# Clustered attention with a Mish FFN: clusters assigned for four heads at once, with block transposes on VectorE and one constant product, and all bulk loads on one queue

## The chip, the cores and the metric

The kernel runs on one core of one Trainium2 chip. The metric is the device time of one execution in microseconds; lower is better. Five engines work beside each other, each through its own list of instructions in order: PE (TensorE, with PEld its weight loads), DVE (VectorE), ACT (ScalarE), POOL (GpSimd) and SP (SyncE, which here only issues DMA transfers). ACT issues DMA transfers too.

## What is computed

Four batches of eight heads, 768 positions, head dimension 64. Each query and key is assigned to one of 16 clusters of its head (largest cosine with a centroid, the first one on a tie); a query attends only to keys of its own cluster. The heads' outputs are joined and go through a two-layer FFN with Mish.

```python
B, H, S, D = q.shape                      # 4, 8, 768, 64
q_assign = np.argmax(np.einsum('bhsd,hcd->bhsc', q_n, c_n), axis=-1)   # 16 clusters
k_assign = np.argmax(np.einsum('bhsd,hcd->bhsc', k_n, c_n), axis=-1)
mask = q_assign[:, :, :, None] == k_assign[:, :, None, :]
scores = np.where(mask, scale * np.matmul(q, k.transpose(0, 1, 3, 2)), -1e9)
attn = softmax(scores)                    # float32 throughout
x = np.matmul(attn, v)                    # -> (3072, 512)
h = x @ w_in                              # 512 -> 2048
g = h * np.tanh(softplus(h))
out = g @ w_out                           # 2048 -> 512
```

`q_n`, `k_n` and `c_n` are the rows divided by their norms.

## The kernel before, in words

**Units.** A head of a batch is numbered n = 0 to 31. Its 768 queries are done in three units of 256, so there are 96 units; unit i has two halves a = 0, 1 of 128 queries. For one half, `scores` makes a 128x768 tile `s` in PSUM (two banks, two buffers with the tag "S"), `rowmax` reduces it on DVE, `expo` takes the exponential on ACT with its sum `l`, `recip` inverts the sum. For the first 24 units (batch 0) `p_lo` transposes P in fp32 on TensorE (tiles `q`, copied to `pt`) and `pv` multiplies with V in fp32 (L588 into 64-column strips of `o`, and L600, which spreads the sums). Later units split P in two fp16 parts (`hl`: POOL L539, DVE L556), transpose them with DMA transposes on SP (`pt`<-`hl`), and L588 is fp16. `pv` does two units at once, each in one half of the array's columns. `pv_out` writes the result to tiles `x`, two fp16 parts.

**FFN.** A step j (of 96) of `m1` makes `h` = w_in-part x `x` (L649 to L651, 24 products of 256 columns), `e_mish`, `e_gh`, `e_gl` make `g`, and `m2` accumulates `O` (L687 to L689, 512 columns). FFN step j stands about 25 units behind attention unit j.

**Weights.** 32 loads (`w_load`, tiles `stage`) bring 64-bit values; ACT (L239) and DVE (L248, L249) turn them into fp32 (`w_abs`, `w_f32`), TensorE sums squares (`w_sq`, tile `gram`), and ACT, POOL and DVE split them in fp16 parts. All this is done during the first 24 units.

**Operands of a head.** `qk_load` brings the raw tile `qk` (128x768: 64 rows of q and 64 of k, 384 KB); `prep_hi` and `prep_lo` scale it (POOL L373, in place) and split it in `A` and `B`; `copy_t`, `copy_z`, `copy_b`, `copy_a` move halves of these into place, by ACT, DVE or DMA. The operands `Z` and `T` have 80 rows: 64 of values and 16 of one-hot clusters, so that the product L493 adds a huge negative number where the clusters differ. These 16 rows are what the change is about.

**The assignment before**, once per head. `assign_mm` (L426): six fp32 products per head, each with a 128x128 piece of the raw tile as the stationary operand and 32 columns of the centroid matrix `C` as the moving one; `C` has for each head 16 columns that see k and 16 that see q. `assign_hot`: DVE takes the maximum of each 16 (L446), compares (L447), a product with `desc` (16 down to 1, POOL or DVE, L453) and a second maximum and compare (L454, L456) leave the first of equal ones. `assign_put`: six bf16 transposes on TensorE (L462), then one ACT instruction (L470) writes the staging tile `stg`, from which `hot_copy` takes the 16 rows to `Z` and to `T` by DMA. For heads 0 and 1 the rows are written directly (L466, L467). The tile "oh" of the transposes is a PSUM buffer that it shares with `o`.

**What sets the order.** A planner (`Plan`) sorts all steps by a time from a table `T` (in units); `pl.after` draws a step's predecessors ahead. Afterwards a scheduler with an estimated timeline sets each engine's list, so that the diff alone doesn't show the order. Bulk loads go to SP or ACT by a fraction in the table (`queue`): all `qk` loads, the w_out stages and half of the w_in stages are issued by ACT.

Of the kernel before, what the change touches and what calls it, by code (L numbers as in the profile page):

```python
# [15 lines left out]
ALU = mybir.AluOpType  # L16
# [39 lines left out]
def tile_clustered_attention_mish_ffn(  # L56
# [13 lines left out]
    raw = pool("raw", 2)  # L70
# [7 lines left out]
    xp = pool("x", 21)  # L78
    mp = pool("moe", 2)
    gp = pool("g", 1)  # L80
    sm = pool("small", 4)
# [11 lines left out]
    def queue(n, kind):  # L93

        f = T["dq", kind]
        if kind == "stage" and n < 8:
            return nc.sync
        return nc.scalar if int((n + 1) * f) != int(n * f) else nc.sync

    last = []  # L100
# [14 lines left out]
    NG, NU, NJ = B * H, B * H * 3, 96  # L115
    units = [(g, qb, g) for g in range(NG) for qb in range(3)]
    uid = {(g, qb): i for i, (g, qb, _) in enumerate(units)}
    first = {}
    for i, (_, _, n) in enumerate(units):
        first.setdefault(n, i)  # L120

# [3 lines left out]
    identb = cp.tile([P, P], BF16, name="identb")  # L125
    nc.vector.tensor_copy(identb, ident)
    ones = cp.tile([P, P], F32, name="ones")
    nc.vector.memset(ones, 1.0)
    desc = cp.tile([P, NCL], F32, name="desc")
    for i in range(NCL):  # L130
        nc.gpsimd.memset(desc[:, i : i + 1], float(NCL - i))
    msc = cp.tile([64, 1], F32, name="msc")
    mbi = cp.tile([64, 1], F32, name="mbi")
    nc.vector.memset(msc[0:32], 1.0)
    nc.vector.memset(msc[32:64], BIG)
    nc.vector.memset(mbi[0:32], 0.0)
    nc.vector.memset(mbi[32:64], -BIG)
# [3 lines left out]
    onehot = [cp.tile([P, 6, 64], BF16, name=f"onehot{i}") for i in range(2)]  # L141
    for o in onehot:
        nc.vector.memset(o, 0.0)


# [34 lines left out]
    def norm_scale(sums, name, pool, tag, largest=False):  # L180
# [5 lines left out]
        if largest:  # L186
# [3 lines left out]
            nc.tensor.matmul(tp[:, :1], ones[:1], m[:1], start=True, stop=True)  # L190
        else:
            nc.tensor.matmul(tp[:, :1], ones, m, start=True, stop=True)
# [20 lines left out]
    def w_load(n):  # L213
# [6 lines left out]
        if i < 8:  # L220
            queue(n, "stage").dma_start(
# [3 lines left out]
        else:  # L225
            r = (n - 16) * P
            queue(n, "stage").dma_start(dst, w_out[r : r + P, :])
# [74 lines left out]
    def v_load(b, hp):  # L302
        t = vp.tile([P, S], F32, tag="v", name=f"vraw{b}_{hp}")
        queue(b * 4 + hp, "v").dma_start(t, vP[b, hp])
        vst[b, hp, "raw"] = t

# [14 lines left out]
    def v_split(b, hp):  # L321
        pl.after(("v_scale", b), ("v_load", b, hp))
        t = vst[b, hp, "raw"]
        if b == 0:
            vst[b, hp] = t.rearrange("p (c h d) -> p c h d", c=6, h=2)
            return
# [37 lines left out]
    def qk_load(n):  # L364
        t = raw.tile([P, S], F32, tag="qk", name=f"qk{n}")
        queue(n, "raw").dma_start(t, qk[n // H, n % H])
        st["qk", n] = t

    def prep_hi(n):
        pl.after(("qk_load", n))  # L370
        r, A = st["qk", n], operand(n, "A")
        if share(n, "f_b", n >= H):
            nc.gpsimd.tensor_scalar(r, r, scq, 1.0, op0=ALU.mult, op1=ALU.mult)  # L373
        sc = 1.0 if share(n, "f_b", n >= H) else scq
        if share(n, "f_a", n >= H):
# [4 lines left out]
    def prep_lo(n):  # L380
        pl.after(("prep_hi", n))
        r, A, Bt = st["qk", n], st["A", n].bitcast(F32), operand(n, "B")
        if share(n, "f_b", n >= H):
# [4 lines left out]
    def copy(n, kind, dst, src):  # L388
# [6 lines left out]
        elif share(n, f"f_{kind}", n >= H):  # L395
# [20 lines left out]
    def assign_mm(n):  # L416
        pl.after(("centroids",), ("qk_load", n))
        h = n % H
        if share(n, "as_o", n >= H):
            o = [ps.tile([P, 512], F32, tag="H", name=f"as{n}_{e}", bufs=2) for e in range(2)]  # L420
        else:
            t = ps2.tile([P, 1024], F32, tag="S", name=f"as{n}")
            o = [t[:, :512], t[:, 512:]]
            st["as", n] = t
        for c in range(6):
            nc.tensor.matmul(  # L426
                o[c // 4][:, c % 4 * P : c % 4 * P + 32], st["qk", n][:, c * P : (c + 1) * P],
                C[:, 32 * h : 32 * h + 32], start=True, stop=True,
            )
        if share(n, "as_o", n >= H):  # L430
            st["as", n] = o

    def assign_hot(n):
        pl.after(("assign_mm", n))
        if n > 1:
# [498 lines left out]
```

## Time and profile before

| what | us |
|---|---|
| median of 3 runs | 992.38 |
| lowest and highest run | 991.54, 995.91 |
| span of the profiled execution | 988.0 |
| the profiled execution's own time | not listed beside its span |
| TensorE busy | 922.7 (93%) |
| VectorE busy | 648.4 (66%) |
| ScalarE busy | 541.3 (55%) |
| GpSimd busy | 430.8 (44%) |

The span is from the first to the last instruction on the core. "Busy" adds up instructions as recorded; those of TensorE are pipelined, so their recorded durations overlap, and what one costs is better read from the distance between two starts. The granted clock is the share of TensorE's full speed that it was given; over the whole span it is 0.976.

### The profile page before, as it was taken

Reading aid. Unit: us, or ns where it says so; the run is one execution under the profiler, and the core shown is the slowest. Engines: PE = TensorE matmul, PEld = TensorE weight load, DVE = VectorE, ACT = ScalarE, POOL = GpSimd, SP = SyncE. Lnnn points to the kernel's source line nnn. Section 1 sums busy time; section 2 is a strip of 40 time slices with the busy share of each in tenths; the row PEclk is TensorE's granted clock in tenths of the full one; section 3 lists DMA queues with packets and bytes.
Section 4 is the critical chain, followed back from the end, with each engine's and each line's share of the span. In section 5 each row is a group of like instructions: output and inputs, shape, how many; then the busy total and the mean of one; then the engine's idle time right before and its main releaser. Section 6 shows DMA issues by size and latency. Waiting matters only on the chain.

```text
span 988.0 us, 17976 instructions
## 1 busy us (share of the span) xinstructions
PE 922.7 (93%) x6913; PEld 665.3 (67%) x6913; DVE 648.4 (66%) x1149; ACT 541.3 (55%) x898; POOL 430.8 (44%) x539
## 2 busy tenths in 40 slices
PE   4998779898999999999999999899999999999997
PEld 3766456676777766767677767667777767676764
DVE  5897976887777767867767777767776776211010
ACT  3676375775666656476756647557566565211111
POOL 3335785426645444654444544644454433111010
PEclk9899788999999999999999999999999999999999
DMA  9735522137796766668577766667657656200000
GB/s 358 227 88 152 175 60 53 39 89 133 134 164 119 157 126 111 130 144 158 116 147 144 149 138 125 125 136 141 134 112 135 118 106 114 43 12 22 12 11 21
DMA packets 250164, 115.49 MB, mean 117 GB/s; under 512 B 229600, under 2 KB 229600, under 8 KB 250080
## 3 DMA queue, kind: packets, MB, share of 16 engines
q1 hardware_dynamic: 238272, 82.50, 43.2%
q10 hardware_dynamic: 11808, 31.86, 11.4%
q8 instruction: 54, 0.88, 0.4%
q14 instruction: 30, 0.25, 0.1%
HBM read 35.68 MB, written 6.29 MB: 42 GB/s over the span
## 4 chain that ended last, share of the span: by engine, by line
PE 22%; ACT 8%; issue 7%; DVE 7%; POOL 5%; DMA 1%; ACTq 0%; POOLq 0%; SPq 0%
PE O L689 3%; PE O L687 3%; PE O L688 3%; PE h L650 3%; PE h L651 3%; PE h L649 3%; POOL hl L539 3%; ACT p L510 2%; DVE m L503 2%; DVE hl L556 2%; ACT u L659 2%; PE o L588 1%; ACT L510 1%; ACT L659 1%; PE s L488 1%
## 5 line engine op out<-in xcount | busy, mean ns | idle before, releaser
L510 ACT ACTIVATE p<-s,m 128x768 f32<-128x768 f32 x192 | 172.7, 900 | 163.7 <-DVE m L503 126.2
L649 PE MATMUL h<-x,w 128*128 128x256 f16 x768 | 212.0, 276 | 2.8 <-ACT x L617 1.5
L650 PE MATMUL h<-x,w 128*128 128x256 f16 x768 | 211.4, 275 | 0.3 <-DVE x L618 0.3
L651 PE MATMUL h<-x,w 128*128 128x256 f16 x768 | 211.5, 275 | 0.0
L556 DVE SCALAR_TENSOR_TENSOR hl<-p,l,hl 128x768 f16<-128x768 f32 x144 | 160.2, 1116 | 61.3 <-POOL hl L539 60.5
L503 DVE TENSOR_REDUCE m<-s 128x1 f32<-128x768 f32 x192 | 181.3, 947 | 18.4 <-PE s L493 16.1
L539 POOL TENSOR_SCALAR hl<-p,l 128x768 f16<-128x768 f32 x144 | 132.4, 921 | 123.9 <-DVE l L521 54.0
L671 DVE SCALAR_TENSOR_TENSOR g<-u,mscg,g 128x512 f16<-128x512 f32 x96 | 78.4, 821 | 132.2 <-POOL g L663 131.3
L663 POOL TENSOR_SCALAR g<-u,mscg 128x512 f16<-128x512 f32 x96 | 79.7, 832 | 177.9 <-ACT u L659 149.1
L687 PE MATMUL O<-w,g 128*128 128x512 f16 x384 | 146.2, 381 | 3.4 <-POOL g L663 2.6
L689 PE MATMUL O<-w,g 128*128 128x512 f16 x384 | 145.8, 380 | 0.9 <-DVE g L671 0.5
L688 PE MATMUL O<-w,g 128*128 128x512 f16 x384 | 145.7, 379 | 0.0
L488 PE MATMUL s<-A,B 128*128 128x384 f32 x384 | 124.6, 406 | 14.9 <-ACT p L510 14.0
L659 ACT ACTIVATE u<-h,msch 128x512 f32<-128x512 f32 x96 | 65.3, 686 | 96.7 <-PE h L651 95.4
L520 POOL TENSOR_SCALAR l<-l 128x1 f32<-128x1 f32 x129 | 43.0, 333 | 170.9 <-ACT p L510 167.5
L493 PE MATMUL s<-Z,T 80*128 80x384 f32 x384 | 103.1, 351 | 3.4 <-ACT T L467 2.5
L649 PEld LDWEIGHTS <-w 128*128 128x128 f16 x768 | 75.9, 99 | 23.8 <-issue 8.4
L488 PEld LDWEIGHTS s<-A,B 128*128 128x128 f32 x384 | 64.4, 195 | 39.1 <-ACT p L510 21.6
L650 PEld LDWEIGHTS <-w 128*128 128x128 f16 x768 | 75.8, 99 | 19.3 <-issue 3.7
L651 PEld LDWEIGHTS <-w 128*128 128x128 f16 x768 | 75.7, 99 | 16.1 <-issue 4.7
L588 PE MATMUL o<-pt,v 128*64 128x256 f16 x1296 | 81.3, 274 | 0.0
L588 PEld LDWEIGHTS <-v 128*64 128x64 f16 x1296 | 68.2, 110 | 14.5 <-issue 12.9
(185 smaller groups left out, 1318.9 us busy)
## 6 DMA issues: line engine op xcount, KB each, us to landing
qk<-in_qk_dram ACTq DMA_DIRECT2D x32, 384.0 KB, 4.2
stage<-in_w_out_dram ACTq DMA_DIRECT2D x16, 512.0 KB, 4.5
vraw<-in_vP_dram SPq DMA_DIRECT2D x16, 384.0 KB, 4.0
out_dram<-osb SPq DMA_DIRECT2D x24, 256.0 KB, 2.3
B<-T ACTq DMA_DIRECT2D x30, 192.0 KB, 4.0
A<-A SPq DMA_DIRECT2D x25, 192.0 KB, 4.6
stage<-in_w_in_dram SPq DMA_DIRECT2D x8, 512.0 KB, 9.4
stage<-in_w_in_dram ACTq DMA_DIRECT2D x8, 512.0 KB, 4.6
```

The lines of the kernel that those rows point to most:

```text
L488: nc.tensor.matmul(s[:, j, :384], st["B", n][:, q0 : q0 + P], st["A", n][:, j * 384 : (j + 1) * 384], start=True, stop=False,)
L503: nc.vector.tensor_reduce(m, st["s", i, a][:, :, :384], axis=AX.XY, op=ALU.max, negate=True)
L510: in_turn(nc.scalar.activation(p.rearrange("p (n x) -> p n x", n=2), st["s", i, a][:, :, :384], AF.Exp, bias=st["m", i, a], scale=1.0, acc ...
L539: nc.gpsimd.tensor_scalar(t[:, 0], p, r, 1.0, op0=ALU.mult, op1=ALU.mult)
L556: nc.vector.scalar_tensor_tensor(t[:, 1], p, r, t[:, 0], op0=ALU.mult, op1=ALU.subtract)
L588: nc.tensor.matmul(o[s * D : s * D + D, :256], v if parts == 1 else v[:, int(part == 1)], st["pt", 2 * m + s][:, :, c + (6 if part == 2 el ...
L649: nc.tensor.matmul(o, wh, xh, start=(c == 0), stop=False)
L650: nc.tensor.matmul(o, wh, xl, start=False, stop=False)
L651: nc.tensor.matmul(o, wl, xh, start=False, stop=(c == 3))
L687: nc.tensor.matmul(o, gh, wh, start=(f == 0 and fi == 0), stop=False)
L688: nc.tensor.matmul(o, gh, wl, start=False, stop=False)
L689: nc.tensor.matmul(o, gl, wh, start=False, stop=(f == 7 and fi == 1))
```

## The change

The assignment is done for a quad of four heads (8 quads instead of 32 heads).

- `assign_mm(q)`: the centroids are now stationary, 32 columns for each of the four heads, in four strips of 32 columns of the array; the raw tiles are the moving operand, 512 and 256 columns. The result has clusters on partitions and positions along the row. So four raw tiles have to be there at once (`raw` has 4 buffers instead of 2), and POOL's scaling in place of these tiles has to wait for the quad's products.
- `assign_hot(q)`: DVE transposes 32x32 blocks, reduces and compares over 48 groups of 16, and transposes the 0/1 result back.
- `assign_put(q)`: one bf16 product with a constant 128x128 matrix `put_w` subtracts the ones of lower index in each group, which leaves the first of equal ones, and scales; DVE takes the maximum with 0 and subtracts `put_b`. `stg` now holds the rows of four heads. `desc`, `onehot`, `msc`, `mbi` and the direct writes for heads 0 and 1 are gone.
- Both PSUM results take a buffer with the tag "S", and the transposed values a buffer of P (`pp`). The staging tile has one buffer, so the last DVE step of a quad waits until the last head of the quad before has been copied.
- `bulk`: all loads of `qk`, `v` and weights are issued by SP, in the order of the plan.
- `pv` waits for V's load instead of its scale in batch 0; the buffers of `x` go from 21 to 18, those of `l` from 12 to 10. The plan's table has new times for the operands' steps. Code for two passes over batch 0 is added and not used (`passes` is 1); with it the unit list, FFN pace and late heads are as before.

```diff
-    raw = pool("raw", 2)
+    raw = pool("raw", T["raw"])
-    xp = pool("x", 21)
+    xp = pool("x", T["xbufs"])
...
+    def bulk(dst, src):
+        made = nc.sync.dma_start(dst, src)
+        if loads:
+            tc.add_manual_dep(made.ins, loads[0], ..., reason="load order")
+        loads[:] = [made.ins.name]
...
+    def put_consts():
+        w = gp.tile([P, P], F32, tag="g", name="put_f")
+        nc.vector.memset(w, -1.0)
...
+        nc.vector.tensor_tensor(w, w, ident, op=ALU.add)
+        nc.vector.tensor_scalar(w4[:, :, 0], w4[:, :, 0], BIG, None, op0=ALU.mult)
+        nc.vector.tensor_copy(put_w, w)
...
-    def assign_mm(n):
-        for c in range(6):
-            nc.tensor.matmul(
-                o[c // 4][:, c % 4 * P : c % 4 * P + 32], st["qk", n][:, c * P : (c + 1) * P],
-                C[:, 32 * h : 32 * h + 32], start=True, stop=True,
+    def assign_mm(q):
+        pl.after(("centroids",), *(("qk_load", n0 + j) for j in range(4)))
+        o = ps2.tile([P, 1024], F32, tag="S", name=f"as{q}")
+        for c0, c1 in ((0, 512), (512, S)):
+            for j in range(4):
+                nc.tensor.matmul(
+                    o[32 * j : 32 * j + 32, c0:c1], C[:, 32 * h : 32 * h + 32], st["qk", n0 + j][:, c0:c1],
+                    start=True, stop=True, skip_group_check=True,
...
+    def assign_hot(q):
+        d = pp.tile([P, S], F32, tag="p", name=f"D{q}")
+        nc.vector.transpose(d, st["as", q][:, :S])
+        nc.vector.tensor_reduce(m, v, axis=AX.X, op=ALU.max)
+        nc.vector.tensor_tensor(hot..., v, m..., op=ALU.is_equal)
+        nc.vector.transpose(t, hot)
+    def assign_put(q):
+        o = ps2.tile([P, 1024], F32, tag="S", name=f"put{q}")
+        for c0, c1 in ((0, 512), (512, S)):
+            nc.tensor.matmul(o[:, c0:c1], put_w, st["hott", q][:, c0:c1], start=True, stop=True)
+        stg = op1.tile([P, S], F32R, tag="stg", name=f"stg{q}")
+        nc.vector.tensor_scalar(stg, o[:, :S], 0.0, put_b, op0=ALU.max, op1=ALU.subtract)
     def qk_load(n):
-        queue(n, "raw").dma_start(t, qk[n // H, n % H])
+        bulk(t, qk[gof[n] // H, gof[n] % H])
...
+    for q, n in owner.items():
+        t = -12 if q == 0 else T["assign1"] if q == 1 and d == 1 else first[n] + T["assign"] * d
```

Where it moves instructions: first TensorE in the stage where attention and FFN run together, at heads 16 and 17 before. `as16` is the assignment product of head 16 (head 16's first piece stands a little earlier), `oh16` its transposes, `s` are scores, `o` is P·V.

```order
L588 MATMUL o20_4379<-pt41_4121,v1_2_2519 64x256
L426 MATMUL as16_4480<-C_142,qk16_4478 128x32 x5
L488 MATMUL s44_1_4487<-A_14_3882,B_14_3897 128x384 x2
L493 MATMUL s44_1_4487<-Z_14_3899,T_14_3885 128x384 x2
...
L426 MATMUL as17_4804<-C_142,qk17_4802 128x32 x3
L462 LDWEIGHTS onehot0_138
L462 MATMUL oh16_4744<-identb_108,onehot0_138 64x128
```

And TensorE at the same heads now: `as4` is the product of the quad of heads 16 to 19, `put4` the constant product, between steps of the FFN (`O`, `h`).

```order
L717 MATMUL O1_1_3797<-w13_1157,g6_3540 128x512
L453 MATMUL as4_4072<-qk16_3984,C_118 32x512
L453 MATMUL as4_4072<-qk17_4066,C_118 32x512
L453 MATMUL as4_4072<-qk18_4068,C_118 32x512
L453 MATMUL as4_4072<-qk19_4070,C_118 32x512
L453 MATMUL as4_4072<-qk16_3984,C_118 32x256
...
L478 MATMUL put4_4212<-hott4_4113,put_w_113 128x512
L478 LDWEIGHTS put_w_113
L478 MATMUL put4_4212<-hott4_4113,put_w_113 128x256
```

One group of eight products and one of two serve four heads, where each head had its own six and six.

Second, ACT while the w_out weights are prepared, before: the `stage` loads stand in its list between the exponentials (`p`), and each waits for its buffer.

```order
L239 ACTIVATE w12_1163<-stage23_1087 128x512
L470 ACTIVATE stg4_1218<-oh4_1211,mbi_130,msc_129 64x768
L227 DMA stage24_1110<-in_w_out_dram 128x512
L227 DMA stage25_1134<-in_w_out_dram 128x512
L227 DMA stage26_1171<-in_w_out_dram 128x512
L239 ACTIVATE w13_1231<-stage24_1110 128x512
L510 ACTIVATE p10_1_1249,l10_1_1250<-s10_1_1242,m10_1_1247 128x768
```

The same loads now, in SP's list, among copies of the heads' operands (`Z`, `T`, `A`).

```order
L108 DMA stage23_1026<-in_w_out_dram 128x512
L108 DMA stage24_1048<-in_w_out_dram 128x512
L108 DMA stage25_1074<-in_w_out_dram 128x512
L108 DMA stage26_1113<-in_w_out_dram 128x512
L108 DMA stage27_1153<-in_w_out_dram 128x512
L493 DMA Z_5_1367<-stg1_939 16x768
L494 DMA T_5_1365<-stg1_939 16x768
```

A load that waits now holds up the copies behind it on SP, no longer ACT's exponentials. Third, SP later, where attention and FFN run together: a raw load stands between the DMA transposes of P.

```order
L587 DMA_TRANSPOSE pt25_2255<-hl25_0_2252 128x12x128
L587 DMA_TRANSPOSE pt25_2255<-hl25_1_2269 128x12x128
L108 DMA qk14_2817<-in_qk_dram 128x768
L587 DMA_TRANSPOSE pt26_2353<-hl26_0_2347 128x12x128
L587 DMA_TRANSPOSE pt26_2353<-hl26_1_2367 128x12x128
```

Before, these raw loads were issued by ACT.

More of the change, by code (lines that the diff above doesn't have):

```diff
@@ L97, in queue @@
             return nc.sync
+        if kind in ("hot", "copy_a", "copy_b") and n < T["act_q"]:
+            return nc.scalar
         return nc.scalar if int((n + 1) * f) != int(n * f) else nc.sync
-    last = []
+    last, loads = [], []
+    def bulk(dst, src):
+        made = nc.sync.dma_start(dst, src)
+        if loads:
+            tc.add_manual_dep(
+                made.ins, loads[0],
+                mybir.DependencyInfo(mybir.DependencyClass.NoSync, mybir.DependencyReason.DATA),
+                reason="load order",
+            )
+        loads[:] = [made.ins.name]
     def in_turn(made):
@@ L117, in tile_clustered_attention_mish_ffn @@
+    gof = {n: g for g, _, n in units}
     uid = {(g, qb): i for i, (g, qb, _) in enumerate(units)}
     first = {}
+    count = {}
     for i, (_, _, n) in enumerate(units):
         first.setdefault(n, i)
+        count[n] = count.get(n, 0) + 1
     ident = cp.tile([P, P], F32, name="ident")
     make_identity(nc, ident)
-    identb = cp.tile([P, P], BF16, name="identb")
-    nc.vector.tensor_copy(identb, ident)
-    ones = cp.tile([P, P], F32, name="ones")
+    ones = cp.tile([P, 1], F32, name="ones")
@@ L128, in tile_clustered_attention_mish_ffn @@
     nc.vector.memset(ones, 1.0)
[L129 to L137, printed above, removed]
+    put_w = cp.tile([P, P], BF16, name="put_w")
+    put_b = cp.tile([P, 1], F32, name="put_b")
@@ L220, in w_load @@
         if i < 8:
-            queue(n, "stage").dma_start(
+            bulk(
                 dst.rearrange("p (c f) -> p c f", c=2),
@@ L226, in w_load @@
             r = (n - 16) * P
-            queue(n, "stage").dma_start(dst, w_out[r : r + P, :])
+            bulk(dst, w_out[r : r + P, :])
     def w_abs(n):
@@ L482, in scores @@
+    def hot_copy(n):
+        q, j = divmod(gof[n], 4)
+        again = T["passes"] == 2 and H <= n < 2 * H
+        pl.after(("assign_put", q), ("copy_t", n), ("copy_z", n))
+        stg, eng = st["kept", q] if again else st["stg", q].bitcast(F32), queue(n, "hot")
+        r = 32 * j
+        eng.dma_start(st["Z", n][D : D + NCL].bitcast(F32), stg[r : r + NCL])
+        eng.dma_start(st["T", n][D : D + NCL].bitcast(F32), stg[r + NCL : r + 2 * NCL])
     def scores(i, a):
@@ L609, in pv_out @@
         b, h = divmod(g, H)
+        if mode(i, 0) == 3:
+            pl.after(("v_scale", b))
         r, r2 = i % 2 * D, h % 2 * D
@@ L806 @@
 T = {
+    'assign1': 2.0,
+    'load1': -2.0,
+    'ffn': [(0, 25.4, 1.0)],
+    'wide': 24,
+    'passes': 1,
+    'v_s0': 30.0,
+    'act_q': 3,
+    'xbufs': 18,
+    'v_sq': 0.5,
+    'assign': -1.4,
+    'lead0': 0.0,
+    'hot_copy': -0.5,
+    'copy_a': -0.57,
+    'copy_b': -0.57,
+    'copy_z': -0.7,
+    'copy_t': -0.73,
+    'prep_lo': -0.8,
+    'prep_hi': -0.87,
+    'load': -1.75,
+    'raw': 4,
     ('f_ws', 0): 0.5,
@@ L846 @@
     ('w_l', 1): 0.7772,
-    'v0': 1.5,
+    'v0': 0.5,
     'v_d': 0.4275,
@@ L867 @@
     'O': 1,
-    'off0': 25.401,
-    'pace': 1.0,
-    ('span', 0): 1.1575,
-    ('span', 1): 1.0762,
-    ('load', 0): -3.8837,
-    ('load', 1): 2.8855,
     ('w0', 0): 0.89,
@@ L883 @@
     ('ws_d', 1): 1.2087,
-    'assign': 0.2164,
-    'hot': 2.2946,
-    'put': 2.3669,
     ('scores', 0): 0.4,
```

217 lines of the change are left out of this document (96 added, 121 removed).

## The prediction

> **What bounds the kernel now.** I read the page's first lines, then cut the span at the first and the last instruction that mix the two halves of the program, then asked in each piece who makes TensorE wait.
>
> ```profile
> span 988.0 us, 17976 instructions
> PE 922.7 (93%) x6913; PEld 665.3 (67%) x6913; DVE 648.4 (66%) x1149; ACT 541.3 (55%) x898; POOL 430.8 (44%) x539
> ```
>
> The cuts are the first FFN product and the last attention product P·V (the first and last starts in these two rows, the second one ending at 853.5):
>
> ```profile
> L649 PE MATMUL h<-x,w x768: 268/273/437, 218.0 to 968.7; 128*128 128x256 f16 x192
> ...
> L588 PE MATMUL o<-pt,v x1296: 272/273/298, 231.3 to 853.2; 128*64 128x256 f16 x186
> ```
>
> ```profile
> 0.00:218.00 218.00, 177.32 (x1167) 132.53 (x1167) 174.99 (x360) 133.17 (x257) 109.49 (x148) 0.91 0.46 140
> 218.00:853.50 635.50, 616.31 (x4883) 448.40 (x4882) 454.44 (x765) 386.78 (x610) 305.44 (x369) 0.99 0.69 131
> 853.50:988.00 134.50, 129.11 (x867) 84.36 (x866) 18.94 (x26) 21.36 (x32) 15.85 (x23) 1.00 0.04 14
> ```
>
> The columns after the length are PE, PEld, DVE, ACT and POOL busy time, then granted clock. Stage A (218 us) is the first 26 units of attention with the preparation of the weights; stage B (635.5) is attention and FFN together; stage C (134.5) is FFN alone. In B TensorE is 97% busy, DVE 72%, ACT 61%, and the longest sum that anything makes TensorE wait there is this:
>
> ```profile
> PE s L488 <- ACT p L510: 11.1, 14, 3.0
> ```
>
> So B is as long as its TensorE work, A is a chain in which DVE is 80% busy and TensorE still idles, and C is untouched by the change.
>
> **TensorE in stage B: the main term.** The old assignment costs what lies between the start of its first product and the start of the next instruction:
>
> ```profile
> 679.60 0.38 PE L689 MATMUL O<-w,g 128*128 128x512 f16 x1
> 679.82 1.42 PE L426 MATMUL as<-C,qk 128*128 128x32 f32 x12
> 681.07 0.59 PE L488 MATMUL s<-A,B 128*128 128x384 f32 x2
> ...
> 515.10 0.52 PE L462 MATMUL oh<-identb,onehot 128*64 128x128 bf16 x6
> 515.55 0.28 PE L650 MATMUL h<-x,w 128*128 128x256 f16 x1
> ```
>
> One head takes 681.07 − 679.82 = 1.25 us for the six fp32 products (two records each) and 515.55 − 515.10 = 0.45 us for the six transposes: 1.70 us. How many heads fall in B:
>
> ```profile
> L426 PE MATMUL as<-C,qk 128*128 128x32 f32 x264 | 32.9, 270 | 0.0
> ```
>
> 264 / 12 = 22 heads, so 22 × 1.70 = 37.4 us leave B.
>
> What comes instead: quads 3 to 7 stand in B by the order of the program, five of eight. Per quad there are eight fp32 products that stream 512 or 256 columns against 32 stationary columns, four strips of the array side by side, and one bf16 product over 768 columns. No row shows four strips. Two strips are shown, by the fp32 P·V of the early units:
>
> ```profile
> 62.05 0.86 PE L588 MATMUL o<-pt,vraw 128*64 128x256 f32 x5
> 62.54 0.38 PE L600 MATMUL o<-ident,l 128*64 128x128 f32 x2
> ...
> 62.76 0.59 PE L600 MATMUL o<-ident,l 128*64 128x128 f32 x4
> ...
> 73.27 1.51 PE L588 MATMUL o<-pt,vraw 128*64 128x256 f32 x12
> 74.72 0.62 PE L488 MATMUL s<-A,B 128*128 128x384 f32 x2
> ```
>
> At 62.5 products of L600 on one strip start while those of L588 run on the other, each strip at its own pace: strips are independent. And 12 records of 256 columns take 74.72 − 73.27 = 1.45 us in two strips, so a record on its strip takes 2 × 1.45 / 12 = 0.24 us for 256 columns. A strip of the new assignment has two records over 768 columns, 2 × 3 × 0.24 = 1.45 us, and if four strips run beside each other that is the quad's time. If only two do, 2.9; if none, 5.8. I take 1.45, because the rows show strips that do not wait for one another, and keep 5.8 as the bad end. The bf16 product costs by L689 above (0.22 us per 512 columns) 0.33. Turning the array from full width to strips and back:
>
> ```profile
> 505.75 0.38 PE L689 MATMUL O<-w,g 128*128 128x512 f16 x1
> 506.06 2.16 PE L588 MATMUL o<-pt,v 128*64 128x256 f16 x36
> 508.15 0.62 PE L488 MATMUL s<-A,B 128*128 128x384 f32 x2
> ```
>
> L588 starts 0.31 us after L689 where 0.22 is its stream, so a turn costs 0.1, two per quad 0.2. Sum per quad 1.45 + 0.33 + 0.2 ≈ 2.0; five quads 10 us. B loses 37.4 − 10 = 27.4 us of TensorE work. TensorE is not quite all of B (97%), and a shorter unit shows a little more of the wait for the exponential; I count nine tenths: −25 us. With two strips at a time it would be 0.9 × (37.4 − 17) = −18, with none −5.
>
> The Trainium skill, "TensorEngine Tiling (Array Packing)", section Key Properties, speaks against the change here: switching the tiling mode drains the array. By the rows above the trace agrees, and the drain is the 0.1 us; the sum would be 1 us better without it. The skill's "TensorE: Matmul & The Clock Gate", section Measured speedup vs the span model, gives 3.07 times for four packed tiles instead of 4; no run here shows it, and by it an estimate of the quad's products is 1.9 us, 2 us more over B.
>
> **The other engines in B.** POOL's product with `desc`, ACT's staging write and DVE's two reduces, compare and one-hot go:
>
> ```profile
> 0.00:218.00 218.00, 19.09 (x40) 0.91 0.46 140
> 218.00:853.50 635.50, 39.88 (x88) 0.99 0.69 131
> ```
>
> This is DVE's time on the tile of maxima (x4 per head): 1.8 us a head in B, 1.9 in A. Per quad DVE now makes two block transposes, a reduce, a compare and the final max-and-subtract, five passes over 128x768. A reduce of that shape is a row; no block transpose is:
>
> ```profile
> L503 DVE TENSOR_REDUCE m<-s 128x1 f32<-128x768 f32 x51 | 48.1, 951 | 15.0 <-PE s L493 13.4 <-ACT rb L627 1.1
> ```
>
> I take 0.95 for all five, 4.75 us a quad (transposes between the same 0.95 and twice it, 6.65 a quad). In B DVE goes from 39.9 to 24 us; it has 28% free there, so nothing is counted. The quad's chain runs about four units ahead of the first scores that need it.
>
> The Trainium skill, "VectorE: DVE Perf Modes", section The three transpose paths, states 311 ns for a 128×128 bf16 transpose on this engine. Six of these are an estimate of 1.9 us per transpose, the upper end above; by it stage A below would be 5 us longer, and the forecast 964 instead of 959.5. No row here shows it.
>
> **Stage A.** Three terms. First the start, which gets longer:
>
> ```profile
> 0.74 0.40 SPq L151 DMA_DIRECT2D csb<-in_cent_dram  x1
> ...
> 3.20 0.22 DVE L154 TENSOR_TENSOR csq<-csb 128x64 f32<-128x64 f32 x1 [0.78 <-DMA csb<-in_cent_dram]
> ...
> 9.47 0.28 DVE L177 COPY C<-ct 64x128 f32<-64x128 f32 x1
> ...
> 21.73 0.96 DVE L503 TENSOR_REDUCE m<-s 128x1 f32<-128x768 f32 x1 [2.89 <-PE s L493]
> ```
>
> ```profile
> GB/s 358 227 88 152 175 60 53 39 89 133 134 164 119 157 126 111 130 144 158 116 147 144 149 138 125 125 136 141 134 112 135 118 106 114 43 12 22 12 11 21
> ```
>
> Now the centroids are the fifth transfer on SP, behind four loads of 384 KB. At 358 GB/s these take 4.4 us, so the centroids land near 6.5 instead of 3.2, and C is ready 6.6 us later (3.20 to 9.75 above), at 13.1. The first products run at half clock (the same twelve records take twice the time of those at 679.82):
>
> ```profile
> 9.90 2.74 PE L426 MATMUL as<-C,qk 128*128 128x32 f32 x12 [0.77 <-DVE C L177]
> ```
>
> So the four strips take 2.9, DVE's four passes 3.9, the product and the last pass 1.6, the copy by DMA about 2.5: 24.0, and two products later the first maximum, near 25.5, against 21.73. POOL comes to the same time: it now scales the raw tiles in place after the assignment has read them, four passes, then A, A and B:
>
> ```profile
> 4.48 0.90 POOL L373 TENSOR_SCALAR qk<-qk,scq 128x768 f32<-128x768 f32 x1 [2.68 <-DMA qk<-in_qk_dram]
> 5.48 0.83 POOL L376 TENSOR_SCALAR A<-qk 128x768 fp32r<-128x768 f32 x1
> 6.39 1.80 POOL L384 TENSOR_TENSOR B<-qk,A 128x768 fp32r<-128x768 f32 x1
> ```
>
> 16 + 3.6 + 1.7 + 1.8 = 23, and the copies after it. So +4.
>
> Second, DVE has three quads to do instead of ten heads: 3 × 4.75 = 14.3 against 19.1 + 1.9 for the two direct copies that also go, −7 on the engine that is 80% busy in A.
>
> Third, the bulk loads leave ACT's queue, where they wait for a staging buffer and hold up what stands behind them:
>
> ```profile
> 100.95 5.88 ACTq L227 DMA_DIRECT2D stage<-in_w_out_dram  x3
> 107.17 0.67 ACT L239 ACTIVATE w<-stage 128x512 f32<-128x512 f32 x1 [5.64 <-DVE w L249]
> ```
>
> Here ACT stands 5.6 us at its own issue while DVE empties the buffer; the exponentials wait behind it. DVE is the slow one at that place, so most of this stays as DVE's time; I count −5. TensorE in A has 10 × 1.7 us less and 3 × 2 more, hidden while DVE leads. A: +4 − 7 − 5 = −8. C: 0.
>
> **Sum.** −25 − 8 = −33 on the profiled execution: 988 − 33 = 955. Its time outside the span isn't listed; the median of the runs, 992.4, lies 4.4 above the span, and I carry that over: 959.5.
>
> **The edits at no cost.** The deeper buffers for raw tiles only let four be held. Eighteen x buffers instead of 21: 12 tiles of a batch live until FFN has read the first third, about 8 units after the batch ends, when the next batch has written six: 18, just enough; without that cover `pv_out` waits one FFN step, 5 us, once a batch. Hot copies for the first three heads go by ACT's queue, which is idle at the start.
>
> **Rivals.** (1) SP's queue makes it slower. The raw loads now stand among the transposes of P:
>
> ```profile
> DMA to landing us min/median/max: 3.6/4.0/7.4
> ...
> L366 ACTq DMA_DIRECT2D qk<-in_qk_dram x20: 329/334/362, 238.4 to 737.8; - x20
> ```
>
> The first row is the landing time of the transposes. 20 loads fall in B; a transpose behind one of them can land one landing later, and what the load waits for holds the queue. It eats the gain when each load holds TensorE for 33 / 20 = 1.65 us; at half a landing, 2 us, plus the waits before it, say 3.5 in all, it is 20 × 3.5 = 70 − 33: about 1030, and just past the point 995 to 1005. For it: the queue is in order. Against it: TensorE waits for no P transpose in the waits of B. (2) The strips don't run beside each other: −5 in B, −8 + 5 in A (two of A's three quads at full clock): 984. Against it: the rows at 62.5. (3) The work leaves but the time doesn't: DVE and the exponential, which make TensorE wait already, take up what it is given, and the start costs what A wins. Then B gives a fifth, −5, A 0: 987 to 992. Against it: 28% of DVE free in B.
>
> **Chances.** My forecast, 948 to 973 (two strips at a time 967; A without its two gains 971; all of B's work, a start no longer than now and twice the gain on ACT's queue, 27 + 17, 948): 0.80. Strips one by one, 984: 0.07. Given back, 987 to 992: 0.06. SP's queue, over 997: 0.07. To hold 8 in 10 the range runs from 946 to 981. Half a per cent, 5 us, is what a measurement of this kernel can tell from none; so faster 0.87 (the first two), same 0.06, slower 0.07.
>
> **What would show it.** Right: the first FFN product near 210; B near 610 with TensorE still 97% busy; eight assignment products of a quad within 1.6 us; C at 134.5; the first maximum near 25. Wrong: products of four strips that start one after another by their full length; TensorE waiting for P's transposes or for Z and T; DVE transposes of several us; ACT or DVE above 90% in B.

## The result and the profile after

The changed kernel takes 983.37 us (median of 4 runs, 982.15 to 984.35), the kernel before 992.99 (4 runs beside it). The ratio is 0.9898 with a 95% interval of 0.9864 to 0.9932: faster by 1.0%, where 3.3% (959.5 us) was forecast. The profiled execution has a span of 981.9 us.

The first lines of its page:

```profile
span 981.9 us, 16957 instructions
PE 890.0 (91%) x6481; PEld 616.4 (63%) x6481; DVE 650.7 (66%) x1052; ACT 515.8 (53%) x866; POOL 423.7 (43%) x498
```

TensorE's busy time is 32.7 us shorter (922.7 before), the span 6.1. The cuts of the stages, from the groups of the first FFN product and of P·V (the last start and its 0.2 us give 847.3):

```profile
L677 PE MATMUL h<-x,w x768: 269/273/421, 221.4 to 962.5; 128*128 128x256 f16 x192
L604 PE MATMUL o<-pt,v x1296: 269/273/423, 234.9 to 847.1; 128*64 128x256 f16 x186
```

The windows of the three stages (PE, PEld, DVE, ACT and POOL busy, then granted clock, DMA share, GB/s):

```profile
0.00:221.40 221.40, 166.43 (x1043) 117.57 (x1044) 171.84 (x330) 125.85 (x245) 106.39 (x128) 0.85 0.45 141
221.40:847.30 625.90, 594.45 (x4574) 414.35 (x4572) 459.87 (x698) 368.59 (x589) 301.42 (x347) 0.98 0.69 132
847.30:981.90 134.60, 129.15 (x867) 84.49 (x866) 19.00 (x26) 21.36 (x32) 15.91 (x23) 1.00 0.04 15
```

| stage | before | forecast | after |
|---|---|---|---|
| A | 218.0 | 210 | 221.4 |
| B | 635.5 | 610 | 625.9 |
| C | 134.5 | 134.5 | 134.6 |

A is 11 us longer than its forecast and 3 longer than before; B is 16 us longer than its forecast and 10 shorter than before. The granted clock in A is 0.91 before and 0.85 now; by x1, x14 and x15 below this is not what A lost. In B TensorE's busy time fell by 21.9 us, but its idle time rose from 635.5 − 616.3 = 19.2 to 625.9 − 594.5 = 31.4. None of the four signs that the prediction names for being wrong appeared: the strips, P's transposes, the DVE transposes and the busy shares of ACT and DVE in B (59% and 73%) are all on the side that it took for right. TensorE's waits in B: the longest is the one of before (11.1 us then), the second has grown (1.3 then), and for P's transposes it waits 0.4 us:

```profile
PE s L503 <- ACT p L525: 16.0, 18, 2.7
PE h L677 <- ACT u L687: 6.8, 9, 1.0
...
PE o L604 <- DMA pt<-hl: 0.4, 1, 0.4
```

The quad itself: the second one, in stage A, at full clock (timeline rows of TensorE and DVE):

```profile
71.92 1.50 PE L453 MATMUL as<-qk,C 128*32 128x512 f32 x16 [0.53 <-ACT p L525]
81.73 0.97 DVE L462 STREAM_TRANSPOSE D<-as 128x768 f32<-128x768 f32 x1
85.56 0.95 DVE L467 TENSOR_TENSOR hot<-D,Dm 128x768 bf16<-128x768 f32 x1
88.57 0.50 PE L478 MATMUL put<-hott,put_w 128*128 128x512 bf16 x2
89.11 1.02 DVE L480 TENSOR_SCALAR stg<-put,put_b 128x768 fp32r<-128x768 f32 x1 [0.34 <-PE put L478]
```

Eight products (16 records) take 1.50 us, so the four strips do run beside each other; the transpose takes 0.97 us. What the forecast has no term for is the 8.3 us between the end of the products (73.42) and the transpose (81.73), and in that time the PSUM buffer of `as` is one that the scores don't have. The third quad, the last in A, has the same gap with 6.3 us; the first, at the start of the kernel, has 0.1. In the five quads of B it is 3.0 to 4.4 us.

```profile
177.37 1.50 PE L453 MATMUL as<-qk,C 128*32 128x512 f32 x16
185.22 0.97 DVE L462 STREAM_TRANSPOSE D<-as 128x768 f32<-128x768 f32 x1
```

### The profile page after: what moved, and what is told of

Its sections match the earlier page's. It is cut to its first block, busy times and chain, and to the rows that moved or that the text cites. A ratio compares the mean times of both kernels' runs of the same rounds, so it can differ in the third digit from the quotient of the medians.

```text
span 981.9 us, 16957 instructions
## 1 busy us (share of the span) xinstructions
PE 890.0 (91%) x6481; PEld 616.4 (63%) x6481; DVE 650.7 (66%) x1052; ACT 515.8 (53%) x866; POOL 423.7 (43%) x498
## 5 line engine op out<-in xcount | busy, mean ns | idle before, releaser
L571 DVE SCALAR_TENSOR_TENSOR hl<-p,l,hl 128x768 f16<-128x768 f32 x144 | 173.2, 1206 | 60.2 <-POOL hl L554 58.7
L554 POOL TENSOR_SCALAR hl<-p,l 128x768 f16<-128x768 f32 x144 | 135.4, 942 | 125.3 <-DVE l L536 41.5
L699 DVE SCALAR_TENSOR_TENSOR g<-u,mscg,g 128x512 f16<-128x512 f32 x96 | 81.8, 856 | 129.4 <-POOL g L691 128.9
L503 PE MATMUL s<-A,B 128*128 128x384 f32 x384 | 128.8, 418 | 25.4 <-ACT p L525 17.5
L535 POOL TENSOR_SCALAR l<-l 128x1 f32<-128x1 f32 x129 | 49.8, 386 | 167.8 <-ACT p L525 162.7
L508 PE MATMUL s<-Z,T 80*128 80x384 f32 x384 | 105.8, 358 | 0.0
L604 PE MATMUL o<-pt,v 128*64 128x256 f16 x1296 | 85.4, 278 | 0.4 <-DMA pt<-hl 0.4
```

Source lines behind the costliest of these rows:

```text
L503: nc.tensor.matmul(s[:, j, :384], st["B", n][:, q0 : q0 + P], st["A", n][:, j * 384 : (j + 1) * 384], start=True, stop=False,)
L554: nc.gpsimd.tensor_scalar(t[:, 0], p, r, 1.0, op0=ALU.mult, op1=ALU.mult)
L571: nc.vector.scalar_tensor_tensor(t[:, 1], p, r, t[:, 0], op0=ALU.mult, op1=ALU.subtract)
L604: nc.tensor.matmul(o[s * D : s * D + D, :256], v if parts == 1 else v[:, int(part == 1)], st["pt", 2 * m + s][:, :, c + (6 if part == 2 el ...
```

## The experiments

Each kernel is timed against the kernel before in the same session; the lengths of the stages are cut as above in its own profile. Nearly every edit also makes the scheduler sort the engines' lists anew. How far it did is read from the traces, by the order in which the instructions of TensorE, DVE, ACT and POOL start, and is said where it matters.

**x1: ACT's wait at the square of V.** ACT's waits of the changed kernel in B showed one that the kernel before does not have:

```profile
ACT vq L343 <- DVE hott L471: 13.8, 4, 4.0
```

```diff
-        junk = gp.tile([P, S], BF16, tag="g", name=f"vq{b}_{hp}")
+        junk = hotp.tile([P, S], BF16, tag="hot", name=f"vq{b}_{hp}")
```

> Only the scratch output of ACT's square of V (vq) moves, from the buffer that it shares with the quad's 0/1 result (hot) to the buffer of the transposed result (hott), which is held for 1 to 2 us instead of about 5. In the changed kernel ACT stands 13.8 us in four places of stage B waiting there, with the exponentials behind it. Theory 1 (what a quad holds up on other engines gives the saved TensorE time back): 6 to 12 us less, near 974 us. Rival (the ring of ACT, POOL and DVE is the bound whatever the quad does): within 3 us of the changed kernel, 983.

Measured: 986.08 us, ratio to before 0.9945 (0.9925 to 0.9965). What the line waits for is now one wait of 3.7 us in the whole span:

```profile
its engine sat idle before it (us, times) until:
  PE put L478: 3.7, 1
```

The wait went and the time did not: B is 628.9. It lay beside other waits, so theory 1 has nothing from this one. A is 219.1 here at a granted clock of 0.91, with D in the same place as in the changed kernel (221.4 at 0.85): the lower clock there is no large part of what A lost.

**x2: another buffer for D in stage A.**

```diff
-        d = pp.tile([P, S], F32, tag="p", name=f"D{q}")
+        d = (hlp.tile([P, S], F32, tag="hl", name=f"D{q}") if q < 3
+             else pp.tile([P, S], F32, tag="p", name=f"D{q}"))
```

> For quads 0 to 2, all in stage A, the transposed values D take a buffer of the fp16 probabilities (not used yet at that time) instead of one of the three buffers of P. Theory 1: the units beside quads 1 and 2, which lose 14.7 and 6.6 us against the kernel before (units 6 to 9 and 18 to 24), get at least half of it back: 8 to 12 us less in A, near 973 us. Rival (what is late there is the quad's data, its place in the order of DVE or a PSUM buffer, not P): 0 to 3 us less.

Measured: 967.46 us, ratio 0.9752 (0.9721 to 0.9784); A 204.5, B 623.3. One line of allocation gives 16.9 us of A; in B TensorE's list kept its order. The same quad's transposed values in x9, a later kernel with the same edit in A, against the rows above:

```profile
70.79 1.50 PE L453 MATMUL as<-qk,C 128*32 128x512 f32 x16 [0.53 <-ACT p L525]
72.50 0.98 DVE L462 STREAM_TRANSPOSE D<-as 128x768 f32<-128x768 f32 x1 [0.76 <-PE as L453]
79.02 0.50 PE L478 MATMUL put<-hott,put_w 128*128 128x512 bf16 x2
```

The transpose comes 0.2 us behind the products, not 8.3. And the exponentials (two records each) that ACT does from 62 to 92 us, in the changed kernel and in x9, by the windows of that line alone:

```profile
62.00:92.00 30.00, 5.96 (x12) 1.00 0.30 99
```

```profile
62.00:92.00 30.00, 8.94 (x18) 1.00 0.54 160
```

Six against nine; the kernel before has ten there. P has three buffers, and in batch 0 they are held through the transposes on TensorE. D, standing in line for one of them, comes late, and holds up `as` and with it the scores. The edit also moves 161 of TensorE's first 919 instructions to other places in its list; x12 and x13 below tell how much that can be worth.

**x3: the loads back on ACT.**

```diff
-        bulk(t, qk[gof[n] // H, gof[n] % H])
+        (nc.scalar.dma_start if n >= 4 else bulk)(t, qk[gof[n] // H, gof[n] % H])
...
-            bulk(dst, w_out[r : r + P, :])
+            nc.scalar.dma_start(dst, w_out[r : r + P, :])
```

> The change without its one order of loads: from the second quad on the raw tiles, half of the w_in stages and all w_out stages go by ACT's queue again, as in the kernel before. If SP's queue had cost what the forecast lacks, stage B would fall by 10 us or more (loads among the transposes of P) and A by the 16.8 us that ACT now waits for stages to land: 965 to 972. If the move of the loads to SP was the gain on ACT that the forecast counted (5 us in A), it is 988. By theory 1 both stages stay within 4 us of the changed kernel.

Measured: 1001.67 us, ratio 1.0102 (1.0065 to 1.0138); A 230.8, B 636.1. In this kernel the loads on SP are no cost but a gain, larger than any of the three expectations had it.

**x4: no quads in B.**

```diff
     def assign_mm(q):
+        if q > 2:
+            return
```

> Leaves out the assignment of heads 12 to 31 altogether (quads 3 to 7: products, DVE passes, constant product, staging write); their rows are copied from the third quad's result. TensorE has 10 us less in B by the forecast's terms. If TensorE's work alone decides (nine tenths of it): 9 us less, 974. By theory 1 the hold-ups of 4 to 5 us per quad go as well: 25 to 32 us less, near 955. If the ring of ACT, POOL and DVE is the bound whatever a quad does: 3 us less, 980.

Measured: 972.45 us, ratio 0.9808 (0.9782 to 0.9835). Its stage B:

```profile
221.90:836.80 614.90, 582.99 (x4485) 413.39 (x4484) 433.14 (x673) 367.02 (x589) 293.73 (x346) 0.98 0.70 134
```

B is 11.0 us shorter, 2.2 per quad, and TensorE's busy time 11.5: near the forecast's 2.0 per quad. But TensorE still idles 614.9 − 583.0 = 31.9 us without any quad. So theory 1 in its first form, that what a quad holds up in B costs 4 to 5 us each, falls: the idle time of B is not the quads' own.

**x5: the loads alone, on the kernel before.**

```diff
-        queue(n, "raw").dma_start(t, qk[n // H, n % H])
+        bulk(t, qk[n // H, n % H])
...
-        queue(b * 4 + hp, "v").dma_start(t, vP[b, hp])
+        bulk(t, vP[b, hp])
```

> The kernel before with one part of the change alone: all loads of raw tiles, V and weights issued by SP in the order of the plan; the assignment per head stays. With the loads back on ACT the changed kernel got 18 us slower, 9 in A and 10 in B. If the loads on SP are worth that by themselves, this kernel takes 973 to 978, and the quads as they stand in the changed kernel add 5 to 10 us to it. If the loads' worth depends on the quads (four raw tiles that are asked for together), it is within 5 us of the kernel before, 988 to 996. If SP's order costs (the first rival of the prediction), over 997.

Measured: 1006.77 us, ratio 1.0133 (1.0068 to 1.0198); A 217.7, B 653.0. Here the loss that the prediction's first rival named is measured: with two raw tiles and one head at a time, loads on SP cost 16 us. Its mechanism is only a small part of it:

```profile
PE as L438 <- DMA qk<-in_qk_dram: 2.7, 2, 1.4
PE o L600 <- DMA pt<-hl: 2.3, 2, 1.3
```

TensorE waits 2.3 us in B for P's transposes and 2.7 for raw tiles, of 17.5 us that B lost. What in SP's order does the rest was not separated; the lists of TensorE and DVE have another order too.

**x6 and x7: less and more TensorE work in B.**

```diff
-            nc.tensor.matmul(o, gh, wl, start=False, stop=False)
+            if k > 8 or f % 2 == 0:
+                nc.tensor.matmul(o, gh, wl, start=False, stop=False)
```

> From here on D has the other buffer of x2 (967.5 us). Leaves out 144 of the 1152 products of the FFN's second layer, all in stage B: 144 x 0.216 = 31 us of TensorE. If B goes by TensorE's work (nine tenths, as the forecast had it): 28 us less, 940. If B is half TensorE and half the ring of ACT, POOL and DVE: 12 to 18 us less, 950 to 956. If the ring is the bound: under 5, 963 or more.

Measured: 952.11 us, ratio 0.9595 (0.9539 to 0.9651): 15.4 less than x2 for 31 us of TensorE.

x7 does the same products a second time instead.

> The same 144 products done twice: 31 us of TensorE more in B. By TensorE's work: 28 to 31 us more, 996 to 998. Half and half: 12 to 20 more, 980 to 987. Ring as the bound: under 8, 975 or less.

Measured: 1007.82 us, ratio 1.0141 (1.0079 to 1.0202): 40 more than x2, more than TensorE's own 31. Stage B of x6 and of x7:

```profile
206.30:817.30 611.00, 564.03 (x4439) 400.37 (x4437) 453.92 (x698) 366.95 (x589) 313.58 (x347) 0.99 0.71 135
```

```profile
205.80:865.30 659.50, 622.98 (x4716) 428.63 (x4714) 454.79 (x698) 368.24 (x589) 290.59 (x347) 0.98 0.65 125
```

Stage B of x2, from which both differ:

```profile
204.50:827.80 623.30, 589.50 (x4575) 412.32 (x4573) 460.70 (x698) 368.53 (x589) 301.48 (x347) 0.99 0.70 132
```

Work that is added costs its full length. Of work that is removed, half comes back as idle time (611.0 − 564.0 = 47.0 us in x6, 623.3 − 589.5 = 33.8 in x2). So there seems to be a bend about where the change puts the kernel. Its size is not certain: in both kernels the order in B changed beside the products (x11 shows what order alone can do there).

**x8: the ring relieved.** ACT changes its function table between the exponential and Mish; the groups of ACT in x2:

```profile
L687 ACT ACT_TABLE_LOAD x36 | 46.2, 1283 | 0.6
L525 ACT ACT_TABLE_LOAD x35 | 44.9, 1283 | 7.9 <-DVE m L518 7.0
```

```diff
-        in_turn(nc.scalar.activation(st["u", j], st["h", j], AF.Mish, scale=vst[j // 24, "h"]))
+        in_turn(nc.scalar.activation(st["u", j], st["h", j], AF.Exp, scale=vst[j // 24, "h"]))
```

> Mish on ACT is replaced by the exponential, so the values are others; what goes is ACT's 71 table loads of 1.28 us (91 us of ACT, nearly all in B), nothing of TensorE. If B goes by TensorE's work it moves by under 5 us (963 to 968). If the ring takes part, B loses more than 10: 940 to 957.

Measured: 935.94 us, ratio 0.9429 (0.9378 to 0.9480), 31.5 less than x2. Stage B and TensorE's longest wait in it:

```profile
205.80:799.10 593.30, 583.82 (x4575) 413.96 (x4573) 463.63 (x698) 271.03 (x519) 303.34 (x347) 0.99 0.72 139
```

```profile
PE s L503 <- ACT p L525: 5.4, 4, 1.7
```

TensorE does the same work and idles 9.5 us, not 33.8. This pair is the cleanest of all: every engine has its instructions in the order of x2, and the exponential takes as long as Mish (683 and 687 ns an instruction), so that nothing but the table loads is gone. The idle time of B comes through ACT, which is only 59% busy there (368.53 of 623.3 us in x2): it is late, not full.

**x10: the same on the kernel before.** The edit is that of x8.

> The kernel before with the exponential in the place of Mish, so without ACT's 71 table loads (91 us of ACT), as x8 was the changed kernel with D moved (935.9 us, B 593.3). If TensorE is the bound of B in the kernel before, as the prediction had it, at most its 19 us of idle time in B go: 975 to 988, B 617 to 630; the change with the ring relieved is then worth 24 us or more in B, which is the forecast's term. If the ring bounds the kernel before as much as the changed one, it falls by 30 like x8: near 960.

Measured: 975.00 us, ratio 0.9848 (0.9810 to 0.9886); its stage B:

```profile
216.80:836.60 619.80, 609.49 (x4882) 447.21 (x4882) 462.56 (x765) 289.69 (x539) 301.39 (x368) 0.99 0.75 134
```

The kernel before has 15.7 us of B from it, x2 has 30.0; here too every list keeps its order. With ACT relieved in both, the change (with D moved in A) is worth 619.8 − 593.3 = 26.5 us in B: the 25 of the forecast. TensorE idles 10.3 us before and 9.5 after. This shows the term and its limit at once.

**x9: D out of P's buffers in B too.** D takes the staging tile's one buffer, which is free once the last head of the quad before has been copied.

```diff
-             else pp.tile([P, S], F32, tag="p", name=f"D{q}"))
+             else op1.tile([P, S], F32, tag="stg", name=f"D{q}"))
```

> x2, and in quads 3 to 7 D takes the buffer of the staging tile, which is free when the last head of the quad before has been copied, so that P keeps its three buffers in B too. In x2 the exponential waits 18.2 us in B behind an instruction of DVE that takes 0.15 us, where the kernel before has 5.8. If that is P's missing buffer: 8 to 15 us less than x2 (967.5), 953 to 960. If the ring is as slow with three buffers: within 3 us of x2. If the staging tile is free too late, D waits and the scores that need the PSUM buffer with it: 3 to 8 us more.

Measured: 958.41 us, ratio 0.9685 (0.9659 to 0.9711), 9.1 less than x2 (7 by the ratios) and the fastest kernel here that does the whole computation (x6 and x8 leave work out):

```profile
0.00:203.60 203.60, 156.95 (x1043) 111.66 (x1044) 167.84 (x330) 124.86 (x245) 109.23 (x128) 0.90 0.50 153
203.60:821.50 617.90, 586.86 (x4574) 412.69 (x4572) 455.51 (x698) 367.81 (x589) 298.01 (x347) 0.99 0.70 134
```

The row that the expectation was built on did not move, though (18.2 in x2):

```profile
ACT p L525 <- DVE l L536: 18.1, 14, 2.1
```

So a gain is there, and the wait that I had read it from was not its sign. Nor does D come much sooner in B: its gap behind the products is 2.8 to 3.5 us for the five quads there, where the changed kernel has 3.0 to 4.4, while in A it went from 8.3 and 6.3 to 0.2 and 0.6. In three places TensorE waits for it, 4.1 us in all:

```profile
PE s L503 <- DVE D L462: 4.1, 3, 1.5
```

TensorE idles 617.9 − 586.9 = 31.0 us in B, as in the changed kernel (31.4) and as in x4 (31.9), where no D is made in B at all. What became shorter there is the recorded busy time of the same products, 594.5 to 586.9, at a granted clock of 0.98 and 0.99, with 368 of TensorE's instructions in other places. That P's buffer is the cause in B is therefore not shown.

**x12: x9 and x1 together.**

> x9 and x1 together. x1 by itself moved nothing (B 628.9 against 625.9), and if ACT's 4 us at vq are covered by its waits for the rowmax, it adds nothing here either: within 3 us of x9. If they were hidden only behind P's missing buffer: 5 to 10 us less than x9.

Measured: 963.94 us, ratio 0.9731 (0.9697 to 0.9762); A 204.7, B 618.9. ACT's wait at the square of V is hidden here as well. The edit moves 137 of TensorE's first 1024 instructions, and A changes by 1.1 us: a new order in A is worth little by itself.

**x13: P's buffer taken away again.** D stays where it is in x9; a tile of P is held in its stead, one column of it in use.

```diff
+        e = pp.tile([P, S], F32, tag="p", name=f"E{q}")
+        nc.vector.tensor_copy(e[:, :1], st["as", q][:, :1])
...
+        nc.vector.tensor_tensor(e1, e[:, :1], hot[:, :1], op=ALU.add)
```

> x9 (958.4 us), with D in its other buffers, but a tile of P taken from where D is written until the 0/1 result is there, with one column written and read (two DVE instructions of 0.1 to 0.2 us per quad more). If P's missing third buffer is what the changed kernel paid, it goes back to the changed kernel: 978 to 986, with stage A near 221. If D's place had another effect (the order of DVE, the time at which D is written): within 4 us of x9.

Measured: 992.51 us, ratio 0.9999 (0.9977 to 1.0022); A 229.7, B 627.9. All that x9 won is gone, 26 us of it in A and 10 in B, with D in its better place. In A the buffer is the cause. The wait is back as well, ten us behind products that begin at 75.16 (the small copy needs P's buffer, and D stands behind it on DVE):

```profile
84.97 0.15 DVE L463 COPY E<-as 128x1 f32<-128x1 f32 x1
85.03 0.97 DVE L464 STREAM_TRANSPOSE D<-as 128x768 f32<-128x768 f32 x1
```

The third quad's gap in A is back too, 7.6 us. Two things come with the held tile, a buffer fewer for the exponentials and a late D that holds `as`; which of them costs the time was not separated. In B the run says less: the exponentials wait 24.9 us there in five places behind the small copy, a wait that the changed kernel does not have. The whole is some 9 us slower than the changed kernel; that the order around it differs is a reason that was not tried.

**x11, x14, x15, x16: the plan's table alone.** One number of the plan's table is moved: P·V from 3.4 to 3.5 (x11 on x2, x16 on the kernel before) or to 3.3 (x14 on x9), the second FFN layer from 3.759 to 3.8 (x15 on x9).

> x2 with one number of the plan's table moved: P·V is asked for a tenth of a unit later (3.5 for 3.4). Nothing is added or removed, so the work on every engine is the same; what moves is the order. It tells how much of a difference of some us in B is order alone. If order matters little: within 3 us of 967.5. If it is as large as what is being explained: 8 us or more either way.

Measured: 995.95 us, ratio 1.0062 (1.0037 to 1.0086), 28 more than x2, all of it in B (656.1).

> x9 with P·V asked for a tenth of a unit earlier in the plan's table (3.3 for 3.4). x11, a tenth later on x2, was 28 us slower, all of it in B, with no work added. If that step was P·V's own place: this one moves by under 5 us or gets faster. If B follows any change of the order by tens of us: 10 to 30 us slower.

Measured: 959.77 us, ratio 0.9659 (0.9630 to 0.9688); A 208.5, B 618.8.

> x9 with the second FFN layer asked for 0.04 unit later (3.8 for 3.759), a change that adds no work and that no theory gives a sign to. It is the spread of order alone on B of x9 (617.9 us): if small, within 4 us of 958.4, and then the 8 us of x2 to x9 and the 10 us of B are what the edits did; if 8 us or more, B's differences of that size in one kernel pair prove nothing.

Measured: 961.25 us, ratio 0.9672 (0.9640 to 0.9705); A 206.0, B 620.2.

> The kernel before with P·V a tenth of a unit later (3.5), the edit of x11. If the changed kernel has less slack in its order than the kernel before, whose TensorE idles 19 us in B: within 8 us of 990. If any kernel of this kind answers so: 15 to 35 us slower, as x11 was.

Measured: 1022.77 us, ratio 1.0306 (1.0279 to 1.0333); A 221.4, B 667.1. A later P·V costs about 30 us in B in either kernel, so that is a matter of this step's place and not of the change. The other two moves changed no order at all: in the traces of x14 and x15 all 6481 instructions of TensorE, and all of DVE, ACT and POOL, start in the order of x9. So they are repeats of x9, and tell the spread of one and the same order over executions: up to 5 us in A, 2 in B, 3 in the whole. Their granted clock in A is 0.93 and 0.97, above the 0.90 of x9, and their A is longer, so the clock doesn't explain A.

The 17 to 26 us that P's buffer makes in A are far outside this spread, and outside the 1 to 2 us that a new order made in A (x12 against x9, x1 against the changed kernel). The 8 to 10 in B (x9 to the changed kernel, and to x13) are outside the spread of repeats, but not outside what order can do there: about 30 us by x11 and x16.

**x17: the loads on ACT beside the repaired quads.** x9 with the edit of x3.

> x9 with raw tiles, half of w_in and w_out loaded by ACT's queue again (the edit of x3). It is the quads alone, repaired, with the loads where they were. x3 was 18 us slower than the changed kernel (A 9, B 10), and the kernel before with its loads on SP 16 us slower (all in B). If loads on SP are worth the same beside the repaired quads: 972 to 980. If x3's loss came with P's missing buffer: within 5 us of x9 (958.4).

Measured: 974.47 us, ratio 0.9840 (0.9812 to 0.9868); A 215.1, B 621.1. One order of loads is worth 16 us here, 11.5 in A and 3.2 in B. Part of A's is the start: DVE waits longer for the centroids, here and in x9:

```profile
12.67 0.23 DVE L184 TENSOR_TENSOR csq<-csb 128x64 f32<-128x64 f32 x1 [11.05 <-DMA csb<-in_cent_dram]
```

```profile
8.04 0.22 DVE L184 TENSOR_TENSOR csq<-csb 128x64 f32<-128x64 f32 x1 [6.41 <-DMA csb<-in_cent_dram]
```

**x18: a cheaper ACT that keeps the result.**

```diff
-    ('f_copy_z', 1): 0.874,
+    ('f_copy_z', 1): 0,
```

> x9 with all copies to Z of later heads made by DMA on SP's queue instead of an ACT instruction of 0.83 us for most heads: about 20 x 0.83 = 17 us less of ACT, 14 of it in B, and as many DMAs more on SP. x8 gave 31 us for 91 us of ACT, so a third: 4 to 5 us less than x9, near 954, and the fastest kernel of the study. Rival: the copies land later among the transposes of P and the scores wait for Z: 5 us or more slower.

Measured: 970.55 us, ratio 0.9814 (0.9776 to 0.9851), 12 more than x9 (A 207.2, B 626.4). The rival's sign was right; whether the copies' landing is what costs was not looked into further. Less ACT time is no gain by itself if it is bought with transfers on SP.

## Why the prediction was wrong, point by point

**The step that failed first** is the part on the other engines and on stage A: D's passes were counted as DVE time, five of them, and the tile that D takes from P's three buffers was given no price at all, although the change says where D lies. It cost 17.8 us in A (changed kernel against x9; x13 shows 26 the other way round). B is 8.0 us shorter in x9 as well, but whether the buffer or the order does that is open. Without the tile in P's buffers A is 203.6, better than the 210 of the forecast, and the kernel takes 958.4, where 959.5 was forecast. That agreement is luck: A is 6.4 us shorter than its forecast there and B 7.9 longer.

**The step that failed second** is the nine tenths in B. The work did leave: between two profiles of the same clock (0.99), TensorE's busy time fell from 616.3 to 586.9 in x9, by 29.4 against 27.4 in the forecast. B fell by 17.6, six tenths, because TensorE's idle time rose from 19.2 to 31.0. I read the 3% of idle time as slack that stays as it is. x6 and x7 point to a bend here, and x8 and x10 show that the idle time comes from ACT's lateness, 71 table changes of it: with those out of the way the change is worth 26.5 us in B. Why ACT is later after the change than before it stays open; by x4 it is not the quads themselves in B. The third rival (the exponential takes up what TensorE is given) named this mechanism and had 28% of free DVE against it; free time on an engine says nothing on how late its next result is. By its number (B −5, A 0) it lay nearer to the result than the forecast, and for A its reason was another.

**A's other terms.** The start: the first maximum came 6.7 us later, not 4 (21.73 before):

```profile
26.13 1.62 PE L503 MATMUL s<-A,B 128*128 128x384 f32 x4 [5.24 <-ACT A L422]
28.43 1.82 DVE L518 TENSOR_REDUCE m<-s 128x1 f32<-128x768 f32 x2 [1.01 <-PE s L508]
```

The quad's chain was on time there: its staging tile is ready at 21.95, against 21.5 in the forecast's sum. What came later is the operand `A`: ACT makes the copy that the scores wait for at 25.24 to 26.07, with squares of V between its copies. The prediction had POOL done at 23 and gave the copies after it no time.

DVE: 7 us less forecast; with the buffer repaired it is 175.0 − 167.8 = 7.2. The loads: 5 us forecast, 11.5 by x17, and my reason (ACT at its own issue) covers only a part, since 4.6 us of the start are in it (12.67 against 8.04 in x17). The loads and the quads need each other: on the kernel before the same move costs 16 us (x5).

**The last term of the sum**, 4.4 us from the span to the median, was too large: the profiled execution of the changed kernel took 983.59 us for a span of 981.9, which is 1.7, and the executions of the kernel before in the later sessions lie 1.9 to 3.4 us above their spans.

**What held.** Four strips beside each other: 1.50 us where 1.45 was taken. Hence the second rival falls, though its number, 984, is the measured one: a time that agrees shows no mechanism. The 2.0 us per quad: 2.2 by x4, though a new order in B is in that number. C: 134.6. The DVE transposes are as the trace's nearest row had them, and the estimate from the Trainium skill, "VectorE: DVE Perf Modes", section The three transpose paths (1.9 us), does not hold here:

```profile
L462 DVE STREAM_TRANSPOSE D<-as x8: 965/969/984, 15.6 to 699.7; 128x768 f32<-128x768 f32 x8
```

The Trainium skill's "TensorE: Matmul & The Clock Gate", section Measured speedup vs the span model, gives 3.07 times for four row tiles; an estimate by it makes the quad's products 1.9 us. The 1.50 above, for four column strips, are against that for this shape. The first rival, SP's queue: TensorE waits 0.4 us for P's transposes in B of the changed kernel, and x17 makes the move a gain there, so it fell; that loads on SP can cost 16 us, x5 shows on the kernel before, but not by TensorE's wait for the transposes.

## What to carry to other kernels

When a change puts a new tile into a pool that another pipeline turns over, price the buffer, not only the passes: ask how long the tile is held, how many buffers are left, and what waits behind the one that comes late. TensorE, 97% busy, was the bound here for work that was added; for work that is removed, ask which result the engine would wait for next, and take the share from a run rather than from the idle time. And a wait that a profile shows in us (13.8 here, at the square of V) is worth nothing until its removal moves the end. Where a scheduler sorts the lists, compare the order in two traces before a difference is put down to the edit: two of the four moves of the plan changed no order, and two others cost 30 us each.

## What was not expected of the hardware

- The block transpose on DVE takes the same 0.97 us for 128x768 in fp32 (above) and in bf16:

```profile
L471 DVE STREAM_TRANSPOSE hott<-hot x8: 962/971/979, 19.0 to 707.9; 128x768 bf16<-128x768 bf16 x8
```

- Four fp32 strips with 32 columns each run at the pace of one: 1.50 us for two records over 768 columns in each, where the two strips of 64 columns in the prediction need 0.24 us per 256 columns, that is 1.45 for the same stream. In this case four strips cost next to no speed against two.
- A change of ACT's function table costs 1.283 us each time, and taking all 71 away was worth 31.5 us on the changed kernel with D moved (x2 to x8) and 15.7 in stage B of the kernel before. The Trainium skill, "ScalarE: Activation LUTs", section What ACT_TABLE_LOAD costs, states about 1283 ns for it: the trace agrees.
